# Linear attention, RMSNorm and a gated feed-forward network on one core: a new order of the steps from block 1 on, and four buffers for the last stores

## The chip, the cores and the metric

The kernel runs on one core of one Trainium2 chip. The metric is the device time of the program in microseconds; less is better. The time before is the median of three runs, 992.07 us (989.55 to 992.15).

## The reference

Linear attention over q, k, v of shape (batch 8, heads 8, sequence 576, width 64); its output is put into 4608 rows (batch and sequence) of 512 (heads and width). On these: RMSNorm and a gated feed-forward network with an inner width of 1536. The weights w_gate, w_val (512 x 1536) and w_out (1536 x 512) arrive as float64, everything else as float32.

```python
q_s = exp(q - max(q, axis=-1)); q_s = q_s / (sum(q_s, axis=-1) + 1e-09)
k_s = exp(k - max(k, axis=2));  k_s = k_s / (sum(k_s, axis=2) + 1e-09)
kv = einsum('bhsd,bhse->bhde', k_s, v)
x = einsum('bhsd,bhde->bhse', q_s, kv)      # then (B,S,H*D) -> (4608, 512)

xn = x / sqrt(mean(x * x, axis=-1) + 1e-06) * rms_g
g = xn @ w_gate
silu = g * (1.0 / (1.0 + exp(-g)))
out = (silu * (xn @ w_val)) @ w_out
```

## The kernel before

The 4608 rows are worked on in nine blocks of 512 tokens. Blocks 0 to 2 use plain matrix products, blocks 3 to 8 go in three pairs with a fast product scheme.

**Plain blocks.** For each block j and each of the twelve chunks i of 128 inner columns there is a step number s = 12 j + i. `f1.s.0` and `f1.s.1` (gate and value) are twelve matmuls of 128 x 512 each (L959): every operand is split into a high and a low fp32r part, and three of the four products are taken. `g_mul` (VectorE, L964) scales the gate out of PSUM, `silu` follows on ScalarE, `h_mul` (VectorE, L971) multiplies it with the value out of PSUM, `h_hi` (a cast, L387) and `h_lo` (a subtraction, L980) split the product, and `f2.s` (twelve matmuls, L996) adds it into four PSUM tiles of the output. Two PSUM banks named `gv` take turns: f1.s.0 gets the bank that g_mul.(s-1) frees, f1.s.1 the one that h_mul.(s-1) frees.

**Pairs.** Pair p holds blocks 3 + 2p and 4 + 2p. For each inner chunk i and for gate and value (m) seven products `pp.p.i.m.k` of six matmuls (L1100) stand in for eight; VectorE combines them out of PSUM (`c_u2`, `c_u3`, `c_21`, `c_22`, `c_12`, all L1121; `c_11`), ScalarE copies the first (`c_s1`) and does the silu, `gate` and `hm` (L1157) form the hidden values, `hp_hi` and `hp_lo` (L1169) split them, and `f2p.p.t.i` (L1187, twelve matmuls) adds block t's chunk into the output tiles. `put.p.t.n` copies a finished output tile n out of PSUM into a buffer `ot` (two of them in turn) and stores its 256 KB from the queue of SyncE (SP, L1193).

**Between them.** The attention of later blocks runs as small steps beside the matmuls. For k the chain is: `k_max` (a column maximum per partition), `k_tr` (a transpose on TensorE, L533), `k_top` (a maximum on VectorE, L538), `k_diag` (on ScalarE, L392, or VectorE, L394), `k_rows` (a small matmul, L547, that spreads the maximum), `k_sub` (VectorE, L553), `k_exp` (ScalarE), `k_mm` (k times v, L565), and then `k_eps`, `k_rec`, `kv_hi`, `kv_lo`. For q: `q_sub`, `q_exp`, `q_sum`, `q_mul`, a transpose `q_t`, the split `q_hi`, `q_lo`, and `q_x` (L771), which gives x. During block 1 the weights are also still split into parts (`w_hi`, `w_lo` L882, `o_hi`, `o_lo` L890, and the sums for the fast scheme, `s_add` L932, `s_hi`, `s_lo` L941) and these go to DRAM (`w_keep`, `o_keep`, `s_keep`); later blocks fetch them again by DMAs that GpSimd issues (`w_in`, `o_in`, `w_back`, `o_back`).

**What sets the order.** A table ORDER lists all 3101 steps by name with their numbers, and behind a colon the engine, where there is a choice: A for ScalarE, D for VectorE, P for GpSimd. The program issues the steps in just this order; each engine and each queue takes its own instructions strictly one after the other, and waits are put in where a step needs another's result or buffer.

Of the kernel before, what the change touches and what calls it, by code (L numbers as in the profile page):

```python
# [90 lines left out]
kv_hi.2.0:D o_lo.12:P k_sub.2.1 s_lo.0.3:P o_hi.13:A h_mul.12 w_hi.14.0.2:A f1.13.1 v_ones.2.2 g_mul.13 s_keep.0.3
o_lo.13:P h_hi.12:A q_max.2.3 k_load.2.2 silu.13 n_cols.1 h_lo.12:P k_exp.2.1 kv_lo.2.0 o_keep.12 store.0.2:D q_x.2.0
s_add.0.4:P k_mm.2.1 x_hi.2.0:A o_keep.13 store.0.3:D h_mul.13 s_hi.0.4:A s_add.1.1:D f2.12 v_ones.2.3 h_hi.13:A
k_eps.2.1 kv_lo.1.3:P v_load.2.2 q_sub.2.1:D s_hi.1.1:A x_sq.2.0 w_lo.14.1:D w_hi.15.0.2:A h_lo.13:D w_lo.14.0:P
f1.14.0 x_lo.2.0 q_exp.2.1 k_max.2.2 o_hi.14:A s_lo.0.4:P w_keep.14 k_rec.2.1 q_max2.2.2 q_sum.2.1 k_load.2.3
s_add.1.2:P f1.14.1 v_load.2.3 o_lo.14:D s_hi.1.2:A kv_hi.2.1:D s_add.1.3:D f2.13 w_lo.15.1:D g_mul.14 s_add.1.4:P
s_keep.0.4 q_half.2.3 silu.14 o_keep.14 w_lo.15.0:P kv_lo.2.1 q_max2.2.3 k_tr.2.2 f1.15.0 k_top.2.2 s_lo.1.1:P
w_keep.15 k_diag.2.2:A h_mul.14 w_hi.16.0.2:A q_half2.2.1 s_lo.1.2:P s_keep.1.1 o_hi.15:A q_sum2.2.1 q_rec.2.1
h_hi.14:A k_rows.2.2 q_mul.2.1:D f1.15.1 s_keep.1.2 s_hi.1.3:A h_lo.14:D w_lo.16.0:D s_lo.1.3:P g_mul.15 k_max.2.3
silu.15 f2.14 w_lo.16.1:P s_keep.1.3 k_sub.2.2 w_hi.17.0.2:A s_add.2.1:P w_keep.16 k_exp.2.2 k_tr.2.3 w_lo.17.0:P  # L100
f1.16.0 k_top.2.3 q_t.2.1 k_diag.2.3:A h_mul.15 q_load.3.0 q_hi.2.1:A w_lo.17.1:D s_hi.1.4:A s_add.2.2:D s_hi.2.1:A
k_mm.2.2 q_lo.2.1:P k_rows.2.3 k_eps.2.2 f1.16.1 k_rec.2.2 k_sub.2.3 kv_hi.2.2:A o_lo.15:D k_exp.2.3 w_keep.17
s_lo.1.4:D s_hi.2.2:A k_load.3.0 h_hi.15:D o_hi.16:A kv_lo.2.2 q_x.2.1 h_lo.15:P g_mul.16 f2.15 s_keep.1.4 x_sq.2.1
v_ones.3.0 s_add.2.3:D silu.16 o_keep.15 s_add.2.4:D q_sub.2.2:D s_add.3.1:D k_mm.2.3 o_lo.16:P f1.17.0 k_eps.2.3
h_mul.16 o_keep.16 s_lo.2.2:D h_hi.16:A s_lo.2.1:D w_hi.18.0.2:A s_keep.2.1 x_hi.2.1:A f1.17.1 w_lo.18.1:D k_load.3.1
w_lo.18.0:P g_mul.17 k_rec.2.3 q_max.3.0 silu.17 h_lo.16:P kv_hi.2.3:A s_keep.2.2 q_half.3.0 f2.16 w_keep.18
w_hi.19.0.2:A q_max2.3.0 q_sub.2.3:P h_mul.17 kv_lo.2.3 o_hi.17:A v_ones.3.1 w_lo.19.1:P q_exp.2.2 f1.18.0 o_lo.17:D
s_hi.2.3:D s_hi.2.4:A o_keep.17 x_acc.2.1:D o_hi.18:A s_lo.2.3:P q_sum.2.2 h_hi.17:A k_max.3.0 f1.18.1 h_lo.17:P
s_keep.2.3 g_mul.18 v_load.3.0 s_add.3.2:D silu.18 s_add.3.3:D f2.17 s_lo.2.4:D q_half2.2.2 q_sub.3.0:P q_exp.2.3
v_load.3.1 h_mul.18 w_lo.19.0:P q_sum2.2.2 q_exp.3.0 q_sum.2.3 f1.19.0 o_lo.18:P h_hi.18:A q_sum.3.0 o_hi.19:A  # L110
q_rec.2.2 w_keep.19 q_half2.2.3 s_hi.3.1:A q_mul.2.2:P s_hi.3.2:A s_keep.2.4 q_sum2.2.3 w_hi.20.0.2:A h_lo.18:P q_t.2.2
f1.19.1 g_mul.19 q_load.3.1 s_add.3.4:P q_rec.2.3 silu.19 w_lo.20.0:D f2.18 w_lo.20.1:D o_lo.19:D q_mul.2.3:P h_mul.19
w_keep.20 h_hi.19:A s_lo.3.2:P q_hi.2.2:A f1.20.0 o_keep.18 s_add.4.1:P o_keep.19 s_keep.3.2 f1.20.1 g_mul.20 q_t.2.3
silu.20 q_lo.2.2:D w_hi.21.0.2:A h_lo.19:D s_hi.3.3:A s_lo.3.1:D f2.19 q_hi.2.3:A w_lo.21.0:D s_keep.3.1 w_hi.22.0.2:A
w_lo.21.1:D q_max.3.1 s_lo.3.3:P w_keep.21 q_half.3.1 f1.21.0 q_load.3.2 s_add.4.2:P q_max2.3.1 h_mul.20 q_lo.2.3:D
# [5 lines left out]
w_hi.24.0.2:A q_sub.3.2:D h_hi.22:A q_mul.3.1:P o_lo.22:P f1.23.1 g_mul.23 q_t.3.1 silu.23 w_lo.24.1:P s_hi.4.3:A
q_load.4.0 h_lo.22:P x_lo.2.1 h_mul.23 w_lo.24.0:P k_tr.3.0 q_x.2.2 k_top.3.0 k_diag.3.0:A k_max.3.1 s_lo.4.3:P
s_hi.4.4:A k_rows.3.0 f2.22 o_keep.22 x_hi.2.2:A k_sub.3.0 x_sq.2.2 q_max.3.3 s_keep.4.3 k_exp.3.0 x_acc.2.2:P x_lo.2.2
q_half.3.3 s_lo.4.2:P q_x.2.3 h_hi.23:A k_tr.3.1 x_hi.2.3:A s_add.5.2:P k_top.3.1 s_keep.4.2 q_max2.3.3 k_diag.3.1:A
x_lo.2.3 x_sq.2.3 k_rows.3.1 q_sub.3.3:P q_exp.3.2 k_sub.3.1 k_mm.3.0 q_max.4.0 x_acc.2.3:P f1.24.0 k_exp.3.1
k_load.3.2 k_eps.3.0 q_sum.3.2 w_hi.25.0.2:A v_ones.3.2 q_half2.3.2 q_exp.3.3 v_load.3.2 w_lo.25.1:P k_rec.3.0
q_half.4.0 kv_hi.3.0:A k_mm.3.1 n_hi.2:A q_max2.4.0 w_lo.25.0:D f1.24.1 q_hi.3.0:A n_lo.2:P k_eps.3.1 o_hi.23:A
k_rec.3.1 kv_lo.3.0 k_load.3.3 kv_hi.3.1:A q_lo.3.0:D v_ones.3.3 s_hi.5.1:A o_lo.23:P kv_lo.3.1 s_hi.5.2:A q_x.3.0
k_max.3.2 w_hi.26.0.2:A q_sub.4.0:P o_keep.23 n_sum.2 x_cp.3.0:A n_t.2 h_lo.23:P f2.23 v_load.3.3 q_hi.3.1:A n_y0.2
x_sq.3.0 q_exp.4.0 q_lo.3.1:P n_y1.2 o_hi.24:A k_tr.3.2 s_lo.4.4:P k_top.3.2 o_lo.24:P s_keep.4.4 store.1.0:A  # L130
k_diag.3.2:A k_max.3.3 store.1.1:A k_rows.3.2 q_x.3.1 o_hi.25:A k_sub.3.2 s_lo.5.1:P q_sum2.3.2 k_exp.3.2 q_rec.3.2
n_rows.2 x_cp.3.1:A q_mul.3.2:P k_mm.3.2 s_keep.5.1 g_mul.24 x_sq.3.1 q_sum.3.3 o_lo.25:P silu.24 q_t.3.2 k_tr.3.3
k_load.4.0 f1.25.0 k_eps.3.2 s_add.5.3:P q_half2.3.3 k_rec.3.2 k_top.3.3 q_load.4.1 v_ones.4.0 k_diag.3.3:D s_hi.5.3:A
h_mul.24 kv_hi.3.2:A s_lo.5.2:D q_hi.3.2:A s_add.5.4:D q_lo.3.2:P k_rows.3.3 x_acc.3.1:P g_mul.25 f1.25.1 v_load.4.0
kv_lo.3.2 k_sub.3.3 q_sum2.3.3 q_rec.3.3 k_max.4.0 q_x.3.2 s_keep.5.2 store.1.2:A s_hi.5.4:A h_hi.24:A h_lo.24:P
s_lo.5.3:P q_sum.4.0 w_lo.26.0:P n_cols.2 s_keep.5.3 store.1.3:A silu.25 k_exp.3.3 f2.24 x_cp.3.2:A x_sq.3.2
q_half2.4.0 w_lo.26.1:P w_hi.27.0.2:A q_sum2.4.0 h_mul.25 q_mul.3.3:P k_tr.4.0 q_max.4.1 k_mm.3.3 k_top.4.0 f1.26.0
q_half.4.1 k_load.4.1 v_ones.4.1 k_diag.4.0:A k_eps.3.3 q_max2.4.1 s_lo.5.4:D q_t.3.3 q_sub.4.1:P s_keep.5.4 q_rec.4.0
q_hi.3.3:A q_mul.4.0:D q_load.4.2 k_rows.4.0 h_hi.25:A f1.26.1 k_rec.3.3 q_lo.3.3:P g_mul.26 o_hi.26:A q_exp.4.1
k_sub.4.0 h_lo.25:P kv_hi.3.3:A q_sum.4.1 k_exp.4.0 q_t.4.0 f2.25 w_lo.27.1:P w_hi.28.0.2:A kv_lo.3.3 k_max.4.1  # L140
q_load.4.3 silu.26 w_lo.28.1:P w_in.0.0.1.2 w_lo.28.0:D k_mm.4.0 o_lo.26:D q_x.3.3 v_ones.4.2 w_lo.27.0:D w_in.0.0.0.2
f1.27.0 h_mul.26 x_cp.3.3:A x_acc.3.2:P v_load.4.1 k_eps.4.0 h_hi.26:A k_rec.4.0 q_half2.4.1 x_sq.3.3 q_sum2.4.1
kv_hi.4.0:A q_rec.4.1 x_acc.3.3:P q_max.4.2 f1.27.1 q_half.4.2 k_load.4.2 q_mul.4.1:P n_hi.3:A kv_lo.4.0 q_hi.4.0:A
w_in.0.0.0.1 h_lo.26:D n_lo.3:P g_mul.27 f2.26 q_t.4.1 silu.27 q_lo.4.0:P o_hi.27:A q_load.5.0 h_mul.27 h_hi.27:A
o_lo.27:P k_tr.4.1 n_sum.3 k_top.4.1 f1.28.0 k_diag.4.1:A n_t.3 q_hi.4.1:A q_max2.4.2 n_y0.3 o_hi.28:A q_sub.4.2:P
# [1090 lines left out]
```

## Time and profile before

| | |
|---|---|
| runs | 992.07 us median (989.55, 992.07, 992.15) |
| profiled execution | 989.84 us, its span 988.1 us |
| granted TensorE clock, mean | 0.985 |
| TensorE matmuls (PE) busy | 950.7 us |
| weight loads (PEld) | 765.5 us |
| VectorE (DVE) | 692.1 us |
| GpSimd (POOL) | 540.3 us |
| ScalarE (ACT) | 449.3 us |

Busy times are sums over the whole span. Times in the views are microseconds from the start of the span. A row of a timeline gives the start, the duration, the instruction and, in brackets, how long its engine was idle before it and on what. L numbers are lines of the kernel before; in the changed kernel the same lines stand one further on (L960 for L959, L1188 for L1187).

### The profile page before, as it was taken

The page shows a single profiled execution, that of the slowest core. Times are in us where ns is not written, and L with a number is a line of the kernel's source. Part 1 is how long each engine was busy: PE and PEld are TensorE (multiplying, and loading weights), DVE is VectorE, ACT ScalarE, POOL GpSimd, SP SyncE. Part 2 cuts the span into 40 slices and gives each one's busy share as a digit, 9 for nine tenths or more (in the row PEclk, how much of TensorE's full clock was granted, in tenths as well). Part 3 has the DMA queues.
Part 4 walks back from the last instruction along what each step waited for, and adds up shares of the span by engine and source line. Part 5 has one row for each costly group of instructions (what it writes and reads, how often), then busy time and mean ns, then how long its engine had stood idle before and what let it go on. Part 6 is the DMA issues. An engine that isn't in the chain of part 4 may idle for free.

```text
span 988.1 us, 14153 instructions
## 1 busy us (share of the span) xinstructions
PE 950.7 (96%) x4681; PEld 765.5 (77%) x4681; DVE 692.1 (70%) x1435; ACT 449.3 (45%) x710; POOL 540.3 (55%) x566
## 2 busy tenths in 40 slices
...
GB/s 235 233 286 194 113 66 237 282 291 261 266 179 245 172 240 185 171 165 262 227 176 248 164 197 168 255 212 214 192 192 149 222 247 225 159 210 196 137 148 172
DMA packets 166692, 202.32 MB, mean 205 GB/s; under 512 B 105908, under 2 KB 127452, under 8 KB 162012
## 3 DMA queue, kind: packets, MB, share of 16 engines
...
## 4 chain that ended last, share of the span: by engine, by line
PE 76%; DVE 8%; DMA 5%; issue 3%; POOL 2%; ACT 2%; SPq 2%; DVEq 0%; ACTq 0%; POOLq 0%
PE ps_gv L1100 17%; PE ps_o L1100 12%; PE ps_gv L959 11%; PE ps_o L1187 10%; PE ps_o L996 6%; PE ps_a L1100 6%; PE ps_a L1187 5%; PE ps_gv L1187 5%; SPq L633 1%; PE ps_a L565 1%; DMA out_dram<-ot 1%; PE ps_a L771 1%; DMA vt<-in_v_dram 1%; POOL w L449 1%; DMA kt<-in_k_dram 1%
## 5 line engine op out<-in xcount | busy, mean ns | idle before, releaser
L959 PE MATMUL ps_gv<-xh,w 128*128 128x512 f32 x576 | 196.1, 407 | 6.6 <-DVE gs L971 3.3
L1100 PE MATMUL ps_gv<-x,ring 128*128 128x512 f32 x576 | 145.2, 396 | 3.5 <-DVE tmp L1121 1.5
L959 PEld LDWEIGHTS ps_gv<-xh,w 128*128 128x128 f32 x576 | 111.2, 193 | 33.6 <-issue 5.2
L1100 PEld LDWEIGHTS ps_gv<-x,ring 128*128 128x128 f32 x576 | 107.7, 189 | 27.3 <-DVE tmp L1121 1.9
L959 PE MATMUL ps_gv<-xl,w 128*128 128x512 f32 x288 | 115.1, 403 | 0.0
L1121 DVE TENSOR_TENSOR tmp<-tmp,ps_gv 128x512 f32<-128x512 f32 x84 | 57.3, 683 | 59.3 <-PE ps_gv L1100 52.3
L1073 POOL DMA_DIRECT2D ring<-wd x54 | 30.6, 566 | 115.8 <-PE ps_gv L1100 54.8
L1100 PE MATMUL ps_o<-x,ring 128*128 128x512 f32 x360 | 84.9, 389 | 0.0
L1100 PEld LDWEIGHTS ps_o<-x,ring 128*128 128x128 f32 x360 | 67.6, 188 | 14.1
L996 PE MATMUL ps_o<-o,hh 128*128 128x512 f32 x256 | 65.4, 397 | 0.0
L959 PEld LDWEIGHTS ps_gv<-xl,w 128*128 128x128 f32 x288 | 56.3, 196 | 11.6 <-issue 0.6
L882 POOL TENSOR_TENSOR w<-w,w 128x512 fp32r<-128x512 f32 x41 | 55.1, 1352 | 8.4 <-ACT w L387 4.2
L1121 DVE TENSOR_TENSOR tmp<-tmp,ps_o 128x512 f32<-128x512 f32 x42 | 28.7, 684 | 40.1 <-PE ps_o L1100 36.9
L387 ACT CAST hh<-gs 128x512 fp32r<-128x512 f32 x47 | 28.9, 616 | 61.3 <-DVE gs L971 24.8
L996 PEld LDWEIGHTS ps_o<-o,hh 128*128 128x128 f32 x256 | 46.9, 188 | 10.2 <-issue 0.4
L1085 POOL DMA_DIRECT2D o<-od x36 | 19.8, 549 | 47.4 <-PE ps_a L1187 22.9
L980 POOL TENSOR_TENSOR hl<-gs,hh 128x512 fp32r<-128x512 f32 x26 | 33.7, 1296 | 14.5 <-ACT hh L387 11.3
L518 DVE TENSOR_REDUCE cm<-kt 116x128 f32<-116x640 f32 x28 | 36.6, 1308 | 5.0 <-DMA kt<-in_k_dram 4.9
L996 PE MATMUL ps_o<-o,hl 128*128 128x512 f32 x128 | 35.3, 398 | 2.1 <-DVE hl L980 2.1
L1187 PE MATMUL ps_o<-o,hh 128*128 128x512 f32 x144 | 37.2, 390 | 0.0
L1100 PE MATMUL ps_a<-x,w 128*128 128x512 f32 x144 | 37.0, 392 | 0.0
L1100 PE MATMUL ps_a<-x,ring 128*128 128x512 f32 x144 | 37.0, 392 | 0.0
...
## 6 DMA issues: line engine op xcount, KB each, us to landing
...
```

The source lines that it names most:

```text
L387: (e.copy if e is nc.scalar else e.tensor_copy)(dst, src)
L449: on(nc.gpsimd).tensor_tensor(out=dst, in0=dst, in1=raw_words(i, a, n, 0), op=ALU.add)
L518: nc.vector.tensor_reduce(out=cm, in_=kt_[b, g].rearrange("p h j d -> p h d j"), axis=AX.X, op=ALU.max)
L882: on(nc.gpsimd).tensor_tensor(out=w[:, :, 1], in0=halves(s % NF, a, 1)[:, 0], in1=w[:, :, 0].bitcast(F32), op=ALU.subtract)
L959: nc.tensor.matmul(pd[s], lhsT=w[:, a, c // 2, m, c % 2 * P:c % 2 * P + P], rhs=X[j, c][x], start=(n == 1), stop=(n == 3 * NKT))
L980: on(nc.gpsimd).tensor_tensor(out=hl, in0=g_[s], in1=h_[s][0].bitcast(F32), op=ALU.subtract)
L996: nc.tensor.matmul(po[t], lhsT=a[:, t * P:(t + 1) * P], rhs=w, start=(i == 0 and n == 0), stop=(i == NF - 1 and n == len(terms) - 1))
L1073: nc.gpsimd.dma_start(t, src.rearrange("p a b f -> p (a b f)"))
L1085: nc.gpsimd.dma_start(WO[n % 4], od[c])
L1100: nc.tensor.matmul(abc[b], lhsT=src[:, h, c * P:(c + 1) * P], rhs=operand(o, c, x), start=first and n == 0, stop=n == 5, skip_group_check= ...
L1121: nc.vector.tensor_tensor(out=dst, in0=ux[u + (src,)], in1=abc[b], op=ALU.add)
L1187: nc.tensor.matmul(pa[p, t, k], lhsT=a[:, k * P:(k + 1) * P], rhs=w, start=(c == 0 and n == 0), stop=(c == NF - 1 and n == 2))
```

## The change

Three things change. No step is added or taken away, and no matmul changes.

1. ORDER is the same up to step 659 (`k_tr.2.0`, about 151 us into the span). From there on all steps are in a new sequence, and many have another engine: two-input steps such as `w_lo`, `s_add`, `s_lo`, `h_lo`, `hp_lo`, `hm` go from GpSimd to VectorE or back, casts and copies (`hp_hi`, `put`, `store`, `c_s1`) between VectorE and ScalarE.
2. The PSUM tiles of the products in the pairs are kept under (pair, chunk, gate or value, bank) instead of the bank alone, so that a later product may take a bank's next tile before the reader of the last one stands in the sequence.
3. In the last block, `put` takes its buffers for tiles 2 and 3 from the pool `gs` (three buffers) instead of `ot`; with the two `ot` there are four. Tile 3 is copied in two halves, the first by ScalarE, the second by VectorE, each with its own store.

```diff
@@ -84,240 +84,241 @@
 q_x0.1.3 h_lo.10:P f2.10 k_max.2.1 x_hi.1.3:A q_sub.2.0:P x_sq.1.3 x_lo.1.3 x_acc.1.3:P q_exp.2.0 q_sum.2.0
...
-k_tr.2.0 h_hi.11:A w_lo.12.1:D f1.12.0 w_lo.13.1:D w_keep.12 k_top.2.0 s_add.0.1:D k_diag.2.0:A w_lo.13.0:D s_hi.0.1:A
...
+k_tr.2.0 k_top.2.0 w_lo.12.1:D f1.12.0 h_hi.11:A q_hi.2.0:A w_lo.13.1:D k_diag.2.0:A w_lo.13.0:D n_t.1 kv_lo.1.2:P
...
@@ -1091,13 +1092,13 @@
         w, o, b = PROD[k]
         first = k in (1, 6, 5)
         if first:
-            abc[b] = ps(BANKS[p % 2][0][b])
+            abc[p, i, m, b] = ps(BANKS[p % 2][0][b])
         tile_ = RING[1][m] if w < A21 else RING[2][m]
         off = w if w < A21 else w - A22
         src = tile_.rearrange("p a b -> p (a b)")[:, off * TB:(off + 1) * TB].rearrange("p (h f) -> p h f", h=2)
         terms = [(0, c, x) for c in range(2) for x in range(2)] + [(1, c, 0) for c in range(2)]
         for n, (h, c, x) in enumerate(terms):
-            nc.tensor.matmul(abc[b], lhsT=src[:, h, c * P:(c + 1) * P], rhs=operand(o, c, x),
+            nc.tensor.matmul(abc[p, i, m, b], lhsT=src[:, h, c * P:(c + 1) * P], rhs=operand(o, c, x),
                              start=first and n == 0, stop=n == 5, skip_group_check=not first)
 
     ux = {}
@@ -1114,11 +1115,11 @@
 
     def c_s1(p, i, m):
         t = ux[p, i, m, 1] = tmp("s")
-        copy(t, abc[0], nc.scalar)
+        copy(t, abc[p, i, m, 0], nc.scalar)
 
     def combine(u, n, dst, src, b):
         ux[u + (n,)] = dst
-        nc.vector.tensor_tensor(out=dst, in0=ux[u + (src,)], in1=abc[b], op=ALU.add)
+        nc.vector.tensor_tensor(out=dst, in0=ux[u + (src,)], in1=abc[u + (b,)], op=ALU.add)
 
     def c_u2(*u):
         combine(u, 2, tmp("u"), 1, 1)
@@ -1132,9 +1133,9 @@
 
     def c_11(p, i, m):
         if m == 0:
-            nc.scalar.activation(g_new(p, 2 * i), abc[0], AF.Silu)
+            nc.scalar.activation(g_new(p, 2 * i), abc[p, i, m, 0], AF.Silu)
         else:
-            nc.vector.tensor_tensor(out=g_[p, 2 * i], in0=abc[0], in1=g_[p, 2 * i], op=ALU.mult)
+            nc.vector.tensor_tensor(out=g_[p, 2 * i], in0=abc[p, i, m, 0], in1=g_[p, 2 * i], op=ALU.mult)
 
     def c_21(p, i, m):
         combine((p, i, m), 21, ux[p, i, m, 1] if m else g_new(p, 2 * i + 1), 1, 1)
@@ -1188,9 +1189,21 @@
                              stop=(c == NF - 1 and n == 2))
 
     def put(p, t, n):
-        ot = fp.tile([P, DM], F32, name="ot", bufs=2)
+        last = p == NPAIR - 1 and t == 1
+        if last and n > 1:
+            ot = fp.tile([P, DM], F32, name="gs", bufs=3)
+        else:
+            ot = fp.tile([P, DM], F32, name="ot", bufs=2)
+        dst = ov[blk(p, t), n]
+        if last and n == T - 1:
+            half = DM // 2
+            nc.scalar.copy(ot[:, :half], pa[p, t, n][:, :half])
+            nc.sync.dma_start(dst[:, :half], ot[:, :half])
+            nc.vector.tensor_copy(ot[:, half:], pa[p, t, n][:, half:])
+            nc.sync.dma_start(dst[:, half:], ot[:, half:])
+            return
         copy(ot, pa[p, t, n], nc.vector if n % 2 else nc.scalar)
-        nc.sync.dma_start(ov[blk(p, t), n], ot)
+        nc.sync.dma_start(dst, ot)
 
     steps = {f.__name__: f for f in (constants, exp_table, conv_add, conv_low, conv_mul, conv_shift, conv_sign, f1, f2, g_load,
               g_mul, h_hi, h_lo, h_mul, k_diag, k_eps, k_exp, k_load, k_max, k_max0, k_mm, k_rec, k_rows, k_sub, k_top,
```

Three places show how the instructions move. First TensorE around the steps `k_tr.3.2` and `k_rows.3.2` (ps_a is a PSUM tile of the attention, cm the column maxima, ps_o the output tiles of f2). Before:

```order
L996 MATMUL ps_o_1919<-o_3014,hl_3055 128x512
L996 MATMUL ps_o_1920<-o_3014,hl_3055 128x512
L533 MATMUL ps_a_3096<-ident_89,cm_3041 128x116
L547 MATMUL ps_a_3096<-cm_3107,ones_91 116x128
L771 MATMUL ps_a_3115<-qh_3074,kv_hi1_102 128x256
L771 MATMUL ps_a_3115<-qh_3074,kv_lo1_103 128x256
L771 MATMUL ps_a_3115<-ql_3083,kv_hi1_102 128x256
L771 MATMUL ps_a_3115<-qh_3074,kv_hi5_110 128x320
```

And in the changed kernel:

```order
L534 MATMUL ps_a_3073<-ident_89,cm_3010 128x116
L997 MATMUL ps_o_1924<-o_2844,hh_3003 128x512 x2
L997 MATMUL ps_o_1925<-o_2844,hh_3003 128x512 x2
L997 MATMUL ps_o_1926<-o_2844,hh_3003 128x512 x2
L997 MATMUL ps_o_1927<-o_2844,hh_3003 128x512 x2
L997 MATMUL ps_o_1924<-o_2844,hl_3029 128x512
L997 MATMUL ps_o_1925<-o_2844,hl_3029 128x512
L997 MATMUL ps_o_1926<-o_2844,hl_3029 128x512
L997 MATMUL ps_o_1927<-o_2844,hl_3029 128x512
L548 MATMUL ps_a_3073<-cm_3101,ones_91 116x128
L772 MATMUL ps_a_3113<-qh_3057,kv_hi1_102 128x256
```

The matmul of `k_rows` stood directly behind the transpose of `k_tr`; now a whole f2 of twelve matmuls stands between them.

Second VectorE between `g_mul.19` and `h_mul.19`, the two steps that free the PSUM banks of step 19 (w, o, sums and parts are weights and their sums in SBUF, qT the transposed q). Before:

```order
L964 TENSOR_TENSOR gs_2494<-ps_gv_2442,r_1782 128x512
L742 RECIPROCAL sm_2473<-sm_2473 128x16
L882 TENSOR_TENSOR w_2475<-w_4_96,w_2475 128x2x256 x2
L890 TENSOR_TENSOR o_2459<-w_3_95,o_2459 128x512
L971 TENSOR_TENSOR gs_2494<-ps_gv_2481,gs_2494 128x512
```

And now, behind `g_mul.19` (L965, gs_2505):

```order
L751 STREAM_TRANSPOSE qT_2507<-qt_1688 128x512
L751 STREAM_TRANSPOSE qT_2510<-qt_1401 128x512
L933 TENSOR_TENSOR sums_1751<-w_3_95,sums_1751 128x512
L891 TENSOR_TENSOR o_2523<-w_3_95,o_2523 128x512
L883 TENSOR_TENSOR w_2450<-w_4_96,w_2450 128x2x256
L933 TENSOR_TENSOR sums_1751<-w_3_95 128x512
L883 TENSOR_TENSOR w_2450<-w_4_96,w_2450 128x2x256
L942 TENSOR_TENSOR parts_1752<-sums_1751,parts_1752 128x2x256
L933 TENSOR_TENSOR sums_1751<-w_4_96 128x512
L761 TENSOR_TENSOR ql_2565<-qT_2510,qh_2540 128x512
L883 TENSOR_TENSOR w_2543<-w_4_96,w_2543 128x2x256
L972 TENSOR_TENSOR gs_2505<-ps_gv_2492,gs_2505 128x512
```

Eleven VectorE steps now stand between the two, where there were four.

Third the end of the program. ScalarE's last instructions (hh the high half of a hidden tile, the others copies of `put`), before:

```order
L1153 ACTIVATE w_5832<-w_5832 128x512
L387 CAST hh_9014<-w_5832 128x512 [waits PE_49,DVE_49,Activation_49,Pool_49]
L387 COPY ot_9016<-ps_o_8082 128x512 [waits DMAHW4_49]
L387 COPY ot_9036<-ps_o_8084 128x512 [waits DMAHW6_49,Activation_49]
L387 COPY ot_9048<-ps_a_8826 128x512 [waits DMAHW0_49,DMAHW2_49,DVE_49,PE_49]
```

And in the changed kernel:

```order
L388 CAST hh_9017<-w_5837 128x512 [waits PE_49,DVE_49,Activation_49,Pool_49]
L1200 COPY gs_9036<-ps_a_8832 128x256 [waits PE_49]
L388 COPY ot_9044<-ps_o_8083 128x512 [waits DMAHW5_49,DMAHW7_49,DMAHW3_49,DVE_49]
L388 COPY ot_9047<-ps_o_8081 128x512 [waits DMAHW6_49,DMAHW2_49,DVE_49]
L388 COPY gs_9050<-ps_gv_8831 128x512
```

ScalarE's copies now begin with the first half of the last tile; two tiles of the pair's first block (ps_o) stand behind it, and a tile of the second block in one of the `gs` buffers last. VectorE's last copies in the changed kernel, in the same order as their stores:

```order
L1170 TENSOR_TENSOR hl_8989<-w_5837,hh_8983 128x512 [waits DVE_49]
L1170 TENSOR_TENSOR hl_9003<-w_5837,hh_8987 128x512 [waits DVE_49,PE_49]
L388 COPY ot_9033<-ps_a_8829 128x512 [waits DMAHW5_49,PE_49]
L1202 COPY gs_9036<-ps_a_8832 128x256 [waits Activation_49]
L388 COPY ot_9041<-ps_gv_8830 128x512 [waits DMAHW6_49,DMAHW4_49,DMAHW2_49]
```

The queue of SP there stores, one after the other, ot_9033, the two halves of gs_9036, ot_9041, ot_9044, ot_9047 and gs_9050.

More of the change, by code (lines that the diff above doesn't have):

```diff
@@ L91 @@
[L91 to L115, printed above, removed]
@@ L121 @@
[L121 to L145, printed above, removed]
```

417 lines of the change are left out of this document (234 added, 183 removed).

## The prediction

> **What bounds the kernel now.** First the page's busy shares and its chain, for the engine that sets the end:
>
> ```profile
> PE   950.7 (96%) x4681; PEld 765.5 (77%) x4681; DVE 692.1 (70%) x1435; ACT 449.3 (45%) x710; POOL 540.3 (55%) x566
> PE 76%; DVE 8%; DMA 5%; issue 3%; POOL 2%; ACT 2%; SPq 2%; DVEq 0%; ACTq 0%; POOLq 0%
> ```
>
> TensorE sets the end, and the change leaves its matmuls as they are. So the question is only how much time in which TensorE does not run at its pace can go. I cut the span where TensorE's own steps end: f2.11 at 159.7, f2.19 at 240.2, f2.24 at 298.2, f2.33 at 392.2; the windows view (busy time of each engine, then the granted clock, DMA share, GB/s) gives:
>
> ```profile
> 159.70:240.20 80.50, 74.31 (x391) 60.17 (x390) 70.17 (x127) 51.00 (x75) 53.50 (x45) 0.98 0.80 277
> 240.20:298.20 58.00, 52.95 (x285) 42.59 (x284) 50.14 (x131) 40.99 (x67) 45.92 (x40) 0.97 0.73 232
> 298.20:392.20 94.00, 89.70 (x518) 72.24 (x517) 82.57 (x218) 61.50 (x96) 69.60 (x77) 0.98 0.83 212
> 392.20:443.00 50.80, 46.89 (x234) 37.45 (x233) 43.88 (x96) 28.10 (x48) 26.02 (x26) 0.93 0.63 172
> 443.00:577.00 134.00, 132.51 (x726) 107.35 (x725) 107.31 (x265) 62.13 (x97) 78.43 (x87) 1.00 0.78 211
> 577.00:976.60 399.60, 399.60 (x1770) 331.18 (x1769) 207.18 (x341) 82.49 (x141) 140.01 (x168) 1.00 0.62 195
> 976.60:988.10 11.50, 5.03 (x23) 3.83 (x21) 2.46 (x4) 1.17 (x2) 0.00 (x0) 0.87 0.43 160
> ```
>
> From 577 to 976.6 TensorE is busy without a gap at clock 1.00: no order can gain there. The chain view shows its pace, 42 matmuls of full length in 9.52 us, 0.227 each:
>
> ```profile
> 638.91 9.52 PE ps_o L1100 x42
> ```
>
> Between 159.7 and 577 TensorE is idle for 6.2 + 5.1 + 4.3 + 3.9 + 1.5 = 20.9 us. The clock column adds to this: (1 - 0.98) x 80.5 + 0.03 x 58 + 0.02 x 94 + 0.07 x 50.8 = 8.8 us. So 29.7 us is all that a new order could win, 14.6 of it up to 298.2 and 15.1 behind. The waits of TensorE after 151 us (total, times, longest) say for what it was idle:
>
> ```profile
> PE ps_a L547 <- ACT cm L392: 4.5, 4, 1.9
> PE ps_gv L959 <- DVE gs L971: 3.3, 2, 2.8
> PE ps_gv L959 <- DVE gs L964: 3.3, 1, 3.3
> PE ps_o L996 <- DVE hl L980: 2.1, 1, 2.1
> PE ps_gv L1100 <- DVE tmp L1121: 1.5, 1, 1.5
> PE ps_a L547 <- DVE cm L394: 1.1, 1, 1.1
> ```
>
> Two kinds: the small matmul of k_rows (L547) that stands right behind its k_tr, and VectorE being late with a product that frees a PSUM bank or feeds f2. Where TensorE starts again, it runs at half pace for a while. TensorE's timeline (start, duration, instruction, idle before):
>
> ```profile
> 186.12 0.47 PE L959 MATMUL ps_gv<-xh,w 128*128 128x512 f32 x1 [3.28 <-DVE gs L964]
> 186.81 0.63 PE L959 MATMUL ps_gv<-xh,w 128*128 128x512 f32 x1
> 187.24 0.63 PE L959 MATMUL ps_gv<-xl,w 128*128 128x512 f32 x1
> 397.44 0.47 PE L547 MATMUL ps_a<-cm,ones 128*116 128x128 f32 x2 [1.90 <-ACT cm L392]
> 398.76 0.63 PE L959 MATMUL ps_gv<-xl,w 128*128 128x512 f32 x1
> 399.18 0.63 PE L959 MATMUL ps_gv<-xh,w 128*128 128x512 f32 x1
> ```
>
> Starts are 0.43 apart instead of 0.227, behind a wait of 3.28 and behind one of only 1.90. The clock is thus charged to short waits too, and I let it go with them in proportion. The Trainium skill says otherwise (TensorE: Matmul & The Clock Gate, "What's actually happening"): the clock halves after about 3.4 us of idle time. The row at 397.44 contradicts it with 1.90, so the measurement decides; by the page's rule none of the 8.8 us would come back with the short waits and my result would be about 4 us later.
>
> **Part 1: k_tr and k_rows apart.** The chain k_tr, k_top, k_diag, k_rows goes through VectorE and ScalarE. In the old order TensorE meets k_rows right after k_tr in several places; the new one puts a whole f1 or f2 between (12 matmuls, 12 x 0.227 = 2.7 us, against a round trip of 285.25 - 283.83 = 1.4):
>
> ```profile
> 283.83 0.26 PE L533 MATMUL ps_a<-ident,cm 116*128 116x116 f32 x1
> 285.25 0.47 PE L547 MATMUL ps_a<-cm,ones 128*116 128x128 f32 x2 [1.16 <-ACT cm L392]
> ```
>
> L547's two waits rows give 4.5 + 1.1 = 5.6 us. I count 4.5 as gone: for k_tr.3.0 the new order has TensorE work enough, for 3.1 and 3.2 an f1 or f2, but k_mm still follows k_rows closely in places, so about 1 stays. Bounds: 0 (if the chain's VectorE part is late anyway) and 5.6.
>
> **Part 2: VectorE's load in block 1.** Between f2.11 and f2.19 the old order gives VectorE 34 and GpSimd 39 two-input steps on SBUF (weight splits, sums, h_lo and the like); the new one 42 and 35. Up to f2.24 it is 51 and 77 against 58 and 65. What one costs, by the groups of the first window (busy, mean ns):
>
> ```profile
> L882 DVE TENSOR_TENSOR w<-w,w 128x512 fp32r<-128x512 f32 x9 | 12.2, 1373 | 0.4 <-ACT w L387 0.4
> L964 DVE TENSOR_TENSOR gs<-ps_gv,r 128x512 f32<-128x512 f32 x8 | 5.5, 683 | 0.7 <-PE ps_gv L959 0.6
> L932 DVE TENSOR_TENSOR sums<-w 128x512 f32<-128x512 f32 x5 | 5.5, 1091 | 0.0
> L980 POOL TENSOR_TENSOR hl<-gs,hh 128x512 fp32r<-128x512 f32 x5 | 6.5, 1294 | 5.0 <-DVE hh L387 3.2 <-ACT hh L387 1.7
> ```
>
> The instruction that reads PSUM (L964) costs 0.68; the same size with both inputs in SBUF costs 1.37 on average. The timelines of both engines show when:
>
> ```profile
> 190.43 0.68 DVE L980 TENSOR_TENSOR hl<-gs,hh 128x512 fp32r<-128x512 f32 x1
> 191.03 1.78 DVE L882 TENSOR_TENSOR w<-w,w 128x512 fp32r<-128x512 f32 x1
> 190.87 1.40 POOL L941 TENSOR_TENSOR parts<-sums,parts 128x512 fp32r<-128x512 f32 x1 [8.00 <-ACT parts L387]
> ```
>
> The first began with GpSimd idle and took 0.68; the second began during GpSimd's own and took 1.78. So eight more on VectorE cost 8 x 0.68 = 5.5 to 8 x 1.37 = 11 us there; the other kinds moved in add about 2. VectorE has 80.5 - 70.2 = 10.3 us of idle time in this window. Up to f2.24 the sum of both engines' two-input work falls: 51 x 0.68 + 77 x 1.3 = 135 us against 58 x 0.68 + 65 x 1.3 = 124 (1.3 as L980 on GpSimd), where TensorE needs 124 (138.5 - 14.6 lost). So the early window gets tighter and the later one looser.
>
> One new place is bad by itself: between g_mul.19 and h_mul.19 the new order has eleven VectorE steps (shown with the change), nine of them two-input on SBUF, where the old had four, three of that kind. The old order's longest such stretch is at g_mul.20:
>
> ```profile
> 234.96 0.69 DVE L964 TENSOR_TENSOR gs<-ps_gv,r 128x512 f32<-128x512 f32 x1 [0.64 <-PE ps_gv L959]
> 237.36 0.69 DVE L941 TENSOR_TENSOR parts<-sums,parts 128x512 fp32r<-128x512 f32 x1
> 237.96 3.48 DVE L882 TENSOR_TENSOR w<-w,w 128x512 fp32r<-128x512 f32 x2
> 242.90 0.68 DVE L971 TENSOR_TENSOR gs<-ps_gv,gs 128x512 f32<-128x512 f32 x1
> ```
>
> There VectorE took 243.6 - 235.0 = 8.6 us, of which TensorE could hide all but 0.7. The new stretch takes 4 x 0.7 + 9 x 0.68 = 8.9 at least and 2.8 + 9 x 1.15 = 13.1 at the window's mixed mean, while TensorE has f1.19.1, f2.18 and f1.20.0, some 41 matmuls, 9.3 us, until f1.20.1 wants that bank. New stall: 0 to 3.8; I take 3 and 1.6 of clock.
>
> Sum up to f2.24: lost before 14.6. Gone: the L964 wait 3.3 and one L971 wait 2.8 with 3 us of clock, two L547 waits (about 2); new: 4.6 and the tighter window, which I put at 1.5. That is -5. Bounds: -11 if VectorE keeps up everywhere, +5 if it does not.
>
> **Part 3: from 298 to 577.** Here both orders load VectorE alike (counted in the two orders from f2.11 on with the rows' unhindered durations: 193 and 197 us up to f2.33, 228 and 225 up to f2.35, where TensorE needs 207 and 239 at its pace). The 15.1 us lost consist of single misfits: h_lo.26 (2.1), the k_rows behind k_tr (about 3), the first products of the pairs (1.5 and some shorter), and 5.4 of clock. The new order separates these pairs; some 3 us of new misfits I allow. I take -8; bounds -14 and 0.
>
> **Part 4: the end.** After 577 VectorE is busy for half of the time (207.2 of 399.6), and reading the new order of pairs 1 and 2 against TensorE's pace I found no new wait of more than 0.5 us. But the last stores move. Before:
>
> ```profile
> 979.63 0.69 DVE L387 COPY ot<-ps_a 128x512 f32<-128x512 f32 x1 [2.64 <-PE ps_a L1187]
> 981.24 0.39 PE L1187 MATMUL ps_a<-o,hl 128*128 128x512 f32 x1
> 982.20 2.05 DMA out_dram<-ot
> 984.35 0.59 ACT L387 COPY ot<-ps_a 128x512 f32<-128x512 f32 x1 [5.07 <-DMA out_dram<-ot]
> 984.96 0.33 SPq L1193 DMA_DIRECT2D out_dram<-ot  x1
> ```
>
> The last matmul ends at P = 981.63; the last copy waits for a store to give its buffer back, and the span ends at P + 6.5. Four buffers take that wait from the last block, but the new order also leaves three full copies behind P on ScalarE: put.2.0.3, put.2.0.1, put.2.1.2. Counted on from P: half copy to 0.5, VectorE's half to 1.0, its put.2.1.1 to 1.65, store landed at 1.65 + 2.03 = 3.7; put.2.0.1 needs that `ot` buffer, copies until 4.3; put.2.1.2 stands behind it on ScalarE, copies until 4.9; its store lands at 6.9, and as before the end follows 1.1 later: P + 8.0. So +1.5; bounds 0 and +2.5. What waits here is the order of the copies, not the number of buffers.
>
> **Rivals.** (a) VectorE's front load decides. In block 1 the extra work, 5.5 + 2 at least, finds no idle time: VectorE's 10.3 us of idle there are waits for its inputs that stay. Then f2.19 comes 7.5 later, half the later relief (2) and a few of the k_rows waits (2) come back, the clock takes 1.5 more, the end 1.5: +6.5, 996. For it: VectorE is busy for 87% of that window and the stretch at g_mul.19. Against: it is two waits in which this window lost its time. It decides once less than 4 us of that idle time can be used. (b) The relief of GpSimd and VectorE works and all waits vanish: -29.7 + 3 left + 1.5 = -25, 965. Against: k_mm behind k_rows stays. (c) Waits only change places, as each removed wait makes the next product late: -1.5 to +1.5 with the end, 990. For it: VectorE's total is unchanged.
>
> **How the numbers follow.** -5 - 8 + 1.5 = -11.5 on the profiled run's 989.84: 978.3. That run is 2.2 under the median of the runs, 992.07, so the new median lies between 978.3 and 980.6; I say 979.5. Chances: this forecast 0.55, (a) 0.21, (b) 0.10, (c) 0.14. Its own range is 970 to 987; to hold 8 in 10, with half of (b) and more than half of (a), it goes from 965 to 998, inside the bounds of the parts (-11 - 14 + 0 = -25 and +5 + 0 + 2.5 = +7.5). A difference counts from 0.3%, 3.0 us, on: faster 0.55 + 0.10 and a little of (c), 0.66; same 0.12; slower 0.22.
>
> **What would show it.** Right: in the new windows idle TensorE time between f2.11 and f2.24 of 7 to 10 us, L548 waits under 1.5 us in all, one wait of some 3 us at f1.20.1 for VectorE's L972, and the span ending about 8 us behind the last matmul. Wrong: f2.19 ending more than 4 us later than 240.2 (then (a)), or TensorE losing less than 6 us in all after 159.7 (then (b)).

## The result

The changed kernel takes 981.73 us (median of four runs, 976.97 to 984.09), the kernel before 991.55 beside it; the ratio is 0.990, 95% interval 0.986 to 0.994. A second set of five runs gave 981.54 against 991.22, ratio 0.990 (0.988 to 0.992). So the change is 1% faster, close to the forecast of 979.5.

The profiled run of the changed kernel took 976.97 us, its span 975.2. Its busy shares on the page:

```profile
PE 944.7 (97%) x4681; PEld 760.8 (78%) x4681; DVE 681.7 (70%) x1436; ACT 456.5 (47%) x721; POOL 524.7 (54%) x557
```

Cut where the same steps of TensorE end as in the prediction (f2.11, f2.19, f2.24, f2.33, then two cuts up to the end of the part with waits, and the last stores), the windows view of the changed kernel reads:

```profile
157.18:230.97 73.79, 73.55 (x398) 60.38 (x399) 65.61 (x141) 51.78 (x82) 44.92 (x42) 1.00 0.86 294
230.97:285.73 54.76, 51.24 (x276) 40.82 (x274) 45.80 (x111) 39.94 (x64) 39.64 (x35) 0.97 0.80 257
285.73:380.30 94.57, 90.17 (x520) 72.86 (x520) 81.67 (x222) 61.20 (x99) 78.23 (x82) 0.98 0.87 214
380.30:430.80 50.50, 49.56 (x263) 40.60 (x262) 41.78 (x102) 32.82 (x49) 33.46 (x35) 1.00 0.75 195
430.80:563.00 132.20, 129.09 (x705) 104.94 (x704) 109.61 (x263) 67.23 (x100) 65.61 (x75) 0.99 0.74 206
563.00:962.10 399.10, 398.02 (x1760) 329.02 (x1759) 208.25 (x340) 79.57 (x136) 134.93 (x165) 1.00 0.62 195
962.10:975.20 13.10, 5.08 (x23) 3.87 (x21) 1.71 (x3) 2.03 (x4) 1.07 (x1) 0.79 0.33 120
```

The first window, block 1, was 80.5 us with 6.2 idle on TensorE and is 73.8 with 0.2 idle. Between f2.11 and 563 TensorE now idles 0.2 + 3.5 + 4.4 + 0.9 + 3.1 = 12.2 us, and the clock column costs 0.03 x 54.8 + 0.02 x 94.6 + 0.01 x 132.2 = 4.9. That is 17.1 lost, against 29.7 before: 12.6 won. The prediction let 13 go. Behind f2p.0.0.11 the change loses 1.2 us on the way to the last matmul, and at the end 1.5. The profiled runs differ by 12.9 us, more than the medians do; 2.7 of it lie ahead of f2.11, almost all where both orders are still the same (f2.11 ends at 156.4 to 160.7 in the profiles of all kernels here, whatever their order).

What TensorE waits for after 151 us in the changed kernel (total, times, longest):

```profile
PE ps_a L566 <- ACT kt L558: 3.9, 4, 2.3
PE ps_a L1101 <- issue: 3.1, 1, 3.1
PE ps_a L566 <- ACT sq L789: 2.2, 1, 2.2
PE ps_a L534 <- DVE cm L519: 0.8, 1, 0.8
PE ps_a L1188 <- DVE hl L1170: 0.8, 1, 0.8
PE ps_gv L960 <- DVE gs L972: 0.2, 1, 0.2
```

The waits of k_rows (L547 before, L548 now), 5.6 us, are gone; so are those of f1 for VectorE's products, but for 0.2 (0.6 at the same place in the second profile). New are waits of k_mm (L566) and one of 3.1 us of a pair's product (L1101) that the view can put down to nothing. The last part, from the timelines of ScalarE and of SP's queue:

```profile
967.21 0.37 ACT L1200 COPY gs<-ps_a 128x256 f32<-128x256 f32 x1 [5.59 <-PE ps_a L1188]
968.00 0.58 ACT L388 COPY ot<-ps_o 128x512 f32<-128x512 f32 x1 [0.41 <-DMA out_dram<-ot]
970.84 0.58 ACT L388 COPY ot<-ps_o 128x512 f32<-128x512 f32 x1 [2.25 <-DMA out_dram<-ot]
971.32 0.59 ACT L388 COPY gs<-ps_gv 128x512 f32<-128x512 f32 x1
```

```profile
971.94 0.33 SPq L1206 DMA_DIRECT2D out_dram<-gs  x1
```

The last matmul ends at P = 967.18; three full copies of ScalarE stand behind it, and the span ends at P + 8.0, as worked out ahead (P + 6.5 before).

### The profile page after: what moved, and what is told of

It is laid out like the page before. It is cut to its first block, busy times and chain, and to the rows that moved or that the text cites. A ratio compares the mean times of both kernels' runs of the same rounds, so it can differ in the third digit from the quotient of the medians.

```text
span 975.2 us, 14167 instructions
## 1 busy us (share of the span) xinstructions
PE 944.7 (97%) x4681; PEld 760.8 (78%) x4681; DVE 681.7 (70%) x1436; ACT 456.5 (47%) x721; POOL 524.7 (54%) x557
## 4 chain that ended last, share of the span: by engine, by line
PE 75%; DMA 8%; DVE 7%; SPq 5%; issue 3%; ACT 1%; POOL 1%; DVEq 0%; ACTq 0%; POOLq 0%
PE ps_gv L1101 17%; PE ps_o L1101 12%; PE ps_gv L960 10%; PE ps_o L1188 10%; PE ps_a L1101 7%; PE ps_o L997 6%; PE ps_a L1188 5%; PE ps_gv L1188 5%; DMA qt<-in_q_dram 3%; SPq L634 2%; DMA kt<-in_k_dram 2%; PE ps_a L566 1%; DMA raw<-in_moe_w_val_dram 1%; SPq L946 1%; PE ps_a L772 1%
## 5 line engine op out<-in xcount | busy, mean ns | idle before, releaser
L960 PE MATMUL ps_gv<-xh,w 128*128 128x512 f32 x576 | 193.2, 402 | 0.2 <-DVE gs L972 0.2
L1101 PE MATMUL ps_gv<-x,ring 128*128 128x512 f32 x576 | 142.2, 392 | 0.0
L960 PEld LDWEIGHTS ps_gv<-xh,w 128*128 128x128 f32 x576 | 108.9, 189 | 26.0 <-issue 1.3
L1101 PEld LDWEIGHTS ps_gv<-x,ring 128*128 128x128 f32 x576 | 107.2, 188 | 22.5
L960 PE MATMUL ps_gv<-xl,w 128*128 128x512 f32 x288 | 112.7, 395 | 0.0
L1101 PE MATMUL ps_o<-x,ring 128*128 128x512 f32 x360 | 84.9, 389 | 0.0
L1101 PEld LDWEIGHTS ps_o<-x,ring 128*128 128x128 f32 x360 | 67.6, 188 | 14.1
L388 ACT CAST hh<-gs 128x512 fp32r<-128x512 f32 x54 | 33.3, 617 | 68.2 <-DVE gs L1138 24.1
L1170 POOL TENSOR_TENSOR hl<-gs,hh 128x512 fp32r<-128x512 f32 x19 | 24.7, 1300 | 29.5 <-PE ps_gv L1101 14.5
L1101 PE MATMUL ps_a<-x,w 128*128 128x512 f32 x144 | 37.0, 392 | 3.1 <-issue 3.1
L388 ACT CAST w<-w 128x1024 fp32r<-128x1024 f32 x30 | 31.3, 1047 | 13.2 <-DMA wd<-w 7.3
L1188 PE MATMUL ps_o<-o,hh 128*128 128x512 f32 x144 | 37.4, 392 | 0.0
L1101 PE MATMUL ps_a<-x,ring 128*128 128x512 f32 x144 | 36.7, 390 | 0.6 <-DVE kt L554 0.6
L1101 PE MATMUL ps_gv<-x,w 128*128 128x512 f32 x144 | 36.8, 403 | 0.0
```

The source lines that it names most:

```text
L388: (e.copy if e is nc.scalar else e.tensor_copy)(dst, src)
L960: nc.tensor.matmul(pd[s], lhsT=w[:, a, c // 2, m, c % 2 * P:c % 2 * P + P], rhs=X[j, c][x], start=(n == 1), stop=(n == 3 * NKT))
L1101: nc.tensor.matmul(abc[p, i, m, b], lhsT=src[:, h, c * P:(c + 1) * P], rhs=operand(o, c, x), start=first and n == 0, stop=n == 5, skip_gro ...
L1170: on(nc.gpsimd).tensor_tensor(out=hl, in0=h_src(p, t, c), in1=HH[p, t, c][0].bitcast(F32), op=ALU.subtract)
L1188: nc.tensor.matmul(pa[p, t, k], lhsT=a[:, k * P:(k + 1) * P], rhs=w, start=(c == 0 and n == 0), stop=(c == NF - 1 and n == 2))
```

## The experiments

In the kernels below whose ORDER is edited, lines stand two further on than in the changed kernel (L566 is L568); in the last of them one. The kernel before ran beside every set; its medians were 989.4 to 991.2. Each set ran beside its own runs of the kernel before, so the ratios compare best across sets. Edits are shown against the changed kernel unless another is named, cut to the steps that matter; "..." marks a cut. The stages below are differences of the times at which TensorE's steps end, from one profile each.

### The new put alone

From step 659 on ORDER is again that of the kernel before; the put stays new.

```diff
-k_tr.2.0 k_top.2.0 w_lo.12.1:D f1.12.0 h_hi.11:A q_hi.2.0:A w_lo.13.1:D k_diag.2.0:A w_lo.13.0:D n_t.1 kv_lo.1.2:P
+k_tr.2.0 h_hi.11:A w_lo.12.1:D f1.12.0 w_lo.13.1:D w_keep.12 k_top.2.0 s_add.0.1:D k_diag.2.0:A w_lo.13.0:D s_hi.0.1:A
...
```

> The old sequence and engines, with only the new put (four buffers in the last block, last tile in halves). Until the last matmul (P) nothing should differ from the kernel before. My theory of the end: with the old sequence only put.2.1.2 and the halves of put.2.1.3 stand behind P, and they need no ot buffer; the last half store would be issued at about P + 1.9 and land 2.05 later, so the span ends at P + 5.0 instead of P + 6.5: 990.1 against 991.55, -1.4 us (-0.15%). Rival, that the four buffers with the halves cost as much themselves as the new end did (P + 8.0): +1.5 us.

988.67 us against 989.89, ratio 0.9985 (0.9969 to 1.0001). P = 983.57, span 988.6: the end is at P + 5.0, as expected. By the end of the span the change of put alone is worth about -1.4; the medians, 1.2 apart, do not by themselves separate that from nothing. The new order turns it into +1.5. The run also shows how much block 1 of the old order varies by itself: f2.11 to f2.19 took 84.3 us here, 80.5 in the profile before, with the same steps.

### New sequence with the old engines, and the reverse

280 steps change their engine between the two orders; two of them in the first edit:

```diff
-s_add.3.4:D
+s_add.3.4:P
...
-s_lo.3.2:D
+s_lo.3.2:P
...
```

> The changed kernel's sequence from block 1 on, but every step on the engine it had before (its new put included). Theory S, the sequence wins: 978 to 985, the stretch of VectorE's two-input steps between f2.11 and f2.19 stays below 6 us (15.4 before, 3.7 in the changed kernel) and TensorE loses under 2 us in that window. Theory E, the move of work from GpSimd to VectorE wins: at least half the gain is lost, 986 or more, with a stretch of over 10 us.

> The old sequence with the engines of the changed kernel (and its put). Theory S: no gain in blocks 1 and 2, 988 to 998, stretch of VectorE's two-input steps between f2.11 and f2.19 over 10 us. Theory E: 985 or less, stretch under 8 us. An order made for other engines may also lose with either, so a loss alone does not tell them apart; the stretch in that window does.

The first took 1000.86 us (ratio 1.010, 1.008 to 1.013), the second 1002.93 (1.013, 1.010 to 1.016): both slower than either order whole. The window from f2.11 to f2.19, new sequence with old engines, then old sequence with new engines:

```profile
157.85:237.16 79.31, 75.15 (x398) 60.04 (x399) 76.30 (x139) 48.47 (x74) 58.08 (x48) 1.00 0.85 289
```

```profile
156.71:237.87 81.16, 75.63 (x391) 60.89 (x390) 68.90 (x129) 53.79 (x82) 45.66 (x40) 0.96 0.80 276
```

What is called stretch in the expectations is, over all of VectorE's two-input steps and casts of 128 x 512 on SBUF, the time beyond 0.683 us each (0.43 for a cast). In this window it sums to 15.4 us over 36 steps in the kernel before, 3.7 over 43 in the changed one, 16.9 over 37 with the old engines, 11.3 over 41 with the old sequence. Neither theory stands. Sequence and engines relieve VectorE only together: with the sequence alone the whole stretch is back, with the engines alone most of it. But block 1 is not where these two lose: from f2.11 to f2.24 they took 137.5 and 141.8 us, no longer than the old order (138.5 to 142.4 in its profiles), and from f2.24 to the last matmul 698.0 and 697.9 against 683.2 before. So in block 1 one half of the new order wins little, and the loss comes behind f2.24; its cause there was not tried. The groups of VectorE in the changed kernel show the relief (busy, mean ns):

```profile
L883 DVE TENSOR_TENSOR w<-w,w 128x512 fp32r<-128x512 f32 x8 | 6.2, 788 | 1.4 <-ACT w L388 1.4
L933 DVE TENSOR_TENSOR sums<-w 128x512 f32<-128x512 f32 x7 | 4.8, 680 | 0.0
L891 DVE TENSOR_TENSOR o<-w,o 128x512 fp32r<-128x512 f32 x4 | 2.7, 679 | 0.0
```

and in the new sequence with the old engines:

```profile
L885 DVE TENSOR_TENSOR w<-w,w 128x512 fp32r<-128x512 f32 x9 | 10.9, 1217 | 0.3 <-ACT w L390 0.3
L935 DVE TENSOR_TENSOR sums<-w 128x512 f32<-128x512 f32 x5 | 5.5, 1104 | 0.0
```

w_lo took 1373 ns in the kernel before, 788 now, 1217 with the old engines.

### GpSimd writes but does not read

```diff
+        if on(nc.gpsimd) is nc.gpsimd and s >= NF:
+            nc.gpsimd.memset(w[:, :, 1].bitcast(F32), 0.0)
+            return
         on(nc.gpsimd).tensor_tensor(
...
```

(On the kernel before; the same in o_lo and s_lo.)

> The kernel before, in which GpSimd's subtractions w_lo, o_lo (from step 12 on) and s_lo are left out and their tiles are set to zero by GpSimd instead: it still writes them, but reads nothing there. The low halves of some weights are thus missing from the result. Theory: what stretched VectorE's two-input steps was GpSimd's reading of the same kind; with about half of GpSimd's 38 two-input steps between f2.11 and f2.19 gone, the stretch there falls from 15.4 to below 7 us and f2.19 comes 4 us or more sooner after f2.11 than 80.5 to 84 us. Rival, VectorE's long steps have another cause (their own operands, DMA traffic): stretch 13 to 16 us, f2.19 within 2 us.

987.43 us against 990.04, ratio 0.998 (0.996 to 1.000). With 18 two-input steps on GpSimd in the window instead of 38, VectorE's stretch there fell from 15.4 to 8.7 us, short of the 7 expected but far from the rival's 13. The window took 78.8 us instead of 80.5 to 84.3, so little of it reached TensorE. Of block 1's two large waits the one for g_mul (L964, here L973) fell from 3.3 to 1.2 us; the one of f1.13.1 for h_mul (L971, here L980) stayed, as the waits view of that window shows:

```profile
PE ps_gv L968 <- DVE gs L980: 3.0, 1, 3.0
PE ps_gv L968 <- DVE gs L973: 1.2, 1, 1.2
```

From f2.19 to f2.24 the run then took 61.2 us instead of 58, so at f2.24 nothing was left of it (140.0 against 138.5 to 142.4). That GpSimd's two-input work stretches VectorE's is thus shown; that block 1's time follows from the stretch alone is not: in three profiles of the old order (before, put alone, and old up to f2.24 below) the stretch was 15.4 us each time, and the window took 80.5, 84.3 and 83.1.

### The changed kernel again, and three single edits of it

> The changed kernel unaltered, as the measure for the three beside it: 981.7 with runs from 977 to 984. The wait of 3.1 us at pp.0.5.1.1 and the end at P + 8.0 should come again; the time lost up to f2.11, where both orders are the same, may differ by some us from the profile before.

981.54 us. The wait at pp.0.5.1.1 (3.1) and the end (P + 8.0) came again.

Early tail:

```diff
 f2p.2.1.3
+put.2.0.3:A
...
 f2p.2.1.6
+put.2.0.1:A
...
 f2p.2.1.11
-put.2.1.0:D put.2.1.3:D put.2.1.1:D put.2.0.3:A put.2.0.1:A put.2.1.2:A
+put.2.1.0:D put.2.1.1:A put.2.1.2:D put.2.1.3:D
```

> The changed kernel with put.2.0.3 and put.2.0.1 moved up behind f2p.2.1.3 and f2p.2.1.6, and the last four copies in the order of their tiles (put.2.1.0, put.2.1.1 on ScalarE, put.2.1.2, the halves of put.2.1.3). Theory, the order of the copies sets the end: the last half store is issued at P + 0.9 and lands at P + 2.9; the span ends at P + 4.0 instead of P + 8.0: -4.0 us against the changed kernel, 977.7. Rival, the end is set by the stores' total traffic: less than -1.

978.41 us, ratio to the kernel before 0.9876 (0.9852 to 0.9901), 3.1 under the changed kernel by the medians, though its runs spread from 976.65 to 983.25. The end in the profile is clearer. Its last copies and stores:

```profile
971.00 0.39 PE L1190 MATMUL ps_a<-o,hl 128*128 128x512 f32 x1
```

```profile
971.42 0.37 ACT L1202 COPY gs<-ps_a 128x256 f32<-128x256 f32 x1 [0.73 <-PE ps_a L1190]
```

```profile
972.39 0.40 SPq L1205 DMA_DIRECT2D out_dram<-gs  x1
```

P = 971.39, span 975.3: P + 3.9. The order of the copies (and, for two of them, the engine, which changed with it) sets the end.

One step back on ScalarE:

```diff
-k_diag.7.3:D
+k_diag.7.3:A
```

> The changed kernel with one step, k_diag.7.3 (a 128 x 128 scaling that took 4.19 us on VectorE at 539.76, 0.28 at its shortest), put back on ScalarE. Theory, this VectorE step stood still while GpSimd ran three two-input steps without a gap, and TensorE's wait of 3.1 us at pp.0.5.1.1 followed from it: -3 us against the changed kernel. Rival, the wait at pp.0.5.1.1 is for the weights' DMA: no change.

976.93 us, ratio 0.985 (0.983 to 0.987), 4.6 under the changed kernel; the wait of 3.1 is gone from its profile, and f2.33 to f2p.0.0.11 took 182.4 us instead of 186.2. This is the wait that the view could name nothing for. VectorE's timeline in the changed kernel:

```profile
539.76 4.19 DVE L395 TENSOR_SCALAR cm<-ident,kx 128x128 f32<-128x128 f32 x1
543.88 0.67 DVE L731 TENSOR_REDUCE sum<-qt 128x16 f32<-128x512 f32 x1
544.47 0.57 DVE L608 SCALAR_TENSOR_TENSOR kv_lo<-ps_a,rs,kv_hi 64x64 fp32r<-64x64 f32 x2
```

and GpSimd's:

```profile
540.12 1.30 POOL L1020 TENSOR_TENSOR xl<-xl,r 128x512 f32<-128x512 f32 x1
541.38 1.27 POOL L1158 TENSOR_TENSOR w<-w,tmp 128x512 f32<-128x512 f32 x1
542.61 1.25 POOL L1170 TENSOR_TENSOR hl<-xh,hh 128x512 fp32r<-128x512 f32 x1
```

A VectorE step that elsewhere takes 0.28 us ends only when GpSimd's third step in a row ends, at 543.9. Behind it stands kv_lo, which reads a PSUM tile of the attention (ps_a); it ends at 545.0, and pp.0.5.1.1 starts in such a tile at 545.1.

Part 1 undone at three places:

```diff
 k_tr.3.1
+k_top.3.1 k_diag.3.1:A k_rows.3.1
...
```

> The changed kernel with part 1 undone at k groups 3.1, 3.2 and 5.3: k_top, k_diag and k_rows directly behind k_tr. Theory: the waits of L548 come back, 1.0 + 1.2 + 1.9 us as in the kernel before, with 1 to 3 us of half clock: +4 to +7 against the changed kernel, 986 to 989. Rival, part 1 is worth nothing as other waits behind it shrink by as much: within 1.5 us.

985.23 us, ratio 0.993 (0.991 to 0.996): +3.7 against the changed kernel, just under the range expected. The waits of k_rows came back, larger than expected:

```profile
PE ps_a L550 <- ACT cm L395: 7.7, 3, 3.9
```

f2.19 to f2.24 took 59.8 us (54.5 in the changed kernel's second profile) and f2.33 to f2p.0.0.11 191.0 (186.2); the stage between gave back 6.4 (90.9 against 97.3). Keeping k_tr and k_rows apart is worth some 4 us, with part of it offset.

### Both repairs, and three more steps moved

> The changed kernel with k_diag.7.3 on ScalarE and with the last copies as in the run with the early tail. If the two are independent, 981.5 - 3.1 - 4.0 = 974.5; no wait of 3 us at pp.0.5.1.1 and the end at P + 4.0. If a new wait takes the place of one, 977 or more.

972.62 us, ratio to the kernel before 0.982 (0.980 to 0.984). The two repairs add up, and no version has a lower median.

```diff
-k_mm.3.0 h_lo.21:D w_lo.23.0:D f2.21
+h_lo.21:D w_lo.23.0:D f2.21 k_mm.3.0
...
```

> As the run with both repairs, and three small matmul steps of TensorE one f1 or f2 later: k_mm.3.0 behind f2.21, n_sum.3 behind f1.28.0, k_mm.5.1 behind f1.33.0. They waited 2.0, 2.1 and 1.8 us in the second profile of the changed kernel, and TensorE ran at half pace behind. Theory, part 3's missing gain sits in such waits for ScalarE and VectorE: -4 to -7 us against the run with both, about 969. Rival, the wait moves on, since their followers (k_eps, kv_hi, q_x) come later too: within 1.5 us of it.

973.80 us, ratio 0.983 (0.981 to 0.985): no gain over the version with both repairs. The waits moved on, but not to the followers that the rival named: f2.21 waits 2.29 us and k_mm.4.1 2.34, and only the third shrank, from 2.31 (k_mm.5.1) to 0.86 (f1.33.1). TensorE's timeline there, where f2.21 and k_mm.3.0 stand:

```profile
251.06 1.20 PE L999 MATMUL ps_o<-o,hl 128*128 128x512 f32 x4 [2.29 <-DVE hl L983]
252.19 0.80 PE L568 MATMUL ps_a<-vt,kt 116*64 116x65 f32 x20
```

f2.21 now waits 2.29 us for its own h_lo.21 where k_mm.3.0 had waited 2.1 ahead of it: the two were late together.

### Where the gain sits

```diff
 f2.24
-q_mul.3.3:D k_exp.3.3 k_max.4.0 s_lo.5.4:P x_cp.3.2:A k_mm.3.3 silu.25
+s_hi.5.3:A k_max.4.0 s_lo.5.3:P q_sum.4.0 n_cols.2 s_keep.5.3 silu.25
...
```

(The new order up to f2.24, the old one behind; then the reverse. At this cut the two orders differ by nine steps only.)

> The new sequence and engines up to f2.24 (1205 steps), behind it the old ones; the new put. Theory, the whole gain sits between f2.11 and f2.24 (138.5 us before, 128.5 in the changed kernel), the rest of the new order gains nothing or loses: f2.11 to f2.24 in 128 to 131 us, from there to the last matmul 683 as before, the end at P + 5.0 as with the old order and the new put: 990 - 10 - 1.4 = 978.6, some 3 us under the changed kernel. Rival, both halves of the new order need each other or share the gain: 983 or more.

> The reverse: the old sequence and engines up to f2.24, behind it the new ones; the new put. Theory: f2.11 to f2.24 in 138 to 143 us, from there to the last matmul 681 to 684, the end at P + 8.0: 990 to 993, no gain. Rival, the new order gains behind f2.24: 987 or less.

982.50 us (ratio 0.993, 0.990 to 0.995) and 987.10 (0.998, 0.996 to 1.001). Both are off the theory: the first by +3.9, the second by -3 to -6, and its ratio does not separate it from the kernel before. The stages in us:

| | old order, new put | new up to f2.24 | old up to f2.24 | new order (profile 1, 2) |
|---|---|---|---|---|
| f2.11 to f2.24 | 142.4 | 129.4 | 141.0 | 128.6, 128.7 |
| f2.24 to f2.33 | 94.0 | 97.4 | 91.4 | 94.6, 97.3 |
| f2.33 to f2p.0.0.11 | 189.7 | 190.4 | 187.3 | 186.2, 186.2 |
| on to P | 399.5 | 399.5 | 400.6 | 400.7, 400.6 |
| P to the end | 5.0 | 5.1 | 7.9 | 8.0, 8.0 |

The stretch from f2.11 to f2.24 (block 1 and the start of block 2) is the gain: three profiles of the old order took 138.5, 142.4 and 141.0 us there, the new one 128.6, 128.7 and, in the first graft, 129.4, so it is worth 9 to 14 us. Behind f2.24 the new order wins 0.2 to 5 us and gives back 1.2 and 3. The 3.4 us that the first graft loses between f2.24 and f2.33 lie at its seam: k_mm there waits 4.16 us for ScalarE.

## Why the prediction was right, by its steps

**The bound and the sum.** TensorE's lost time was the right account: 29.7 us before, 17.1 now, 12.6 won where the sum took 13. The time, 981.7, lies 2.2 from 979.5, and -9.8 stands against -11.5. But the parts were off in opposite directions, and that is partly luck. Of the four signs set out for being right, two came (no waits of k_rows, the end at P + 8.0) and two did not: between f2.11 and f2.24 TensorE was idle for 3.7 us, not 7 to 10, and no wait of 3 us stood at f1.20.1.

**Part 1, k_tr and k_rows.** Right: the waits are gone (0, forecast under 1.5 us), and put back they cost 3.7 us. What remains is in k_mm, as said.

**Part 2, VectorE's load in block 1.** The step that failed is the price of the moved steps, "5.5 to 11 us", and with it "the early window gets tighter": the sum's terms 4.6 (stall and clock) and 1.5 (tighter window) measured next to nothing. Eight more two-input steps on VectorE made it less busy, 65.6 us instead of 70.2, as the stretch fell from 15.4 to 3.7. The unhindered price, 0.68, was the right one for nearly all; I took the mean of the old order for a property of the step, when it was one of what ran beside it. The stall of 3 us at f1.20.1 did not come: 0.2 in the first profile, 0.6 in the second. There all nine two-input steps took 0.65 to 0.69 us; from the start of g_mul.19 to the end of h_mul.19 VectorE took 9.4 us, of which 1.4 were a wait for ScalarE. (Setting the two engines' summed work, 135 and 124 us, against TensorE's 124 bounded nothing, since they run side by side; and the wait behind g_mul.20 was 0.56 us, not 0.7.) Up to f2.24 the change won 10 us in the first profiles, not 5, and 9 to 14 with the other profiles: about the bound of -11.

**Part 3, 298 to 577.** Oversized: -8 forecast, -3.0 in the first profile and -0.2 in the second (283.8 before, 280.8 and 283.5 now). The old misfits went, but I had allowed 3 us of new ones; a wait of k_mm (2.3), the 3.1 at pp.0.5.1.1 and the clock behind f2.24 (0.02 x 94.6 + 0.01 x 132.2 = 3.2) are 8.6. One engine letter makes 3 of them.

**Part 4, the end.** P + 8.0 forecast and measured. That it hangs on the order of the copies is shown by the early tail (P + 3.9) and the put alone (P + 5.0). After 577 I had found no wait above 0.5; 1.2 us came, 0.8 of it the wait of L1188 shown above.

**Rivals.** (a) fell with the price of part 2. (b) holds in block 1 alone, where the waits did vanish. (c) describes what happened behind f2.24.

**The clock.** Charging it to short waits in proportion came out in the sum (17.1 against 29.7 includes 4.9 against 8.8), but only as an average: the same wait of 1.90 us that the prediction shows halved the clock in some profiles and not in others, as shown below.
